# DiT block on one core: the MLP gate taken off TensorE and summed on VectorE and GpSimd

## The chip, the cores and the metric

The kernel runs on one core of a Trainium2 chip. The metric is the device time of one execution in microseconds (us); lower is better. A core has five engines with instruction queues of their own: TensorE (PE in the profile; its weight loads are PEld), VectorE (DVE), ScalarE (ACT), GpSimd (POOL) and SyncE (SP), which here issues most of the transfers (DMAs). They meet through semaphores.

## The reference

One transformer block whose normalisations are shifted and scaled, and whose two branches are gated, by six vectors per batch computed from `c`. B = 2, N = 256, D = 1152, two heads of 576, and an MLP of width F = 4608; everything is bf16.

```python
mod = (silu(c) @ w_mod).reshape(B, 6, 1, D)
shift_a, scale_a, gate_a, shift_m, scale_m, gate_m = [mod[:, i] for i in range(6)]
h = layernorm(x) * (1 + scale_a) + shift_a
q, k, v = split(h @ wqkv)
attn = softmax(einsum('bqhd,bkhd->bhqk', q, k) * Dh ** -0.5)
a = einsum('bhqk,bkhd->bqhd', attn, v).reshape(B, N, D) @ wo
x = x + gate_a * a
h2 = layernorm(x) * (1 + scale_m) + shift_m
m = gelu(h2 @ w_fc1) @ w_fc2
return x + gate_m * m
```

## The kernel before, in words

**The planner.** The kernel first collects its work as units, each with an engine, an estimated cost in ns and the memory that it reads and writes. `Sched._track` (L229) derives the dependences from that: in SBUF by overlapping bytes, in PSUM by whole banks (a VectorE read of a bank waits for the last TensorE unit that wrote to it). TensorE and SyncE keep the order in which the code lists their units. VectorE, ScalarE and GpSimd are ordered by a list scheduler (`schedule`, L281) with the given costs, save for a hand-written start on VectorE and ScalarE (`S.first`, L907). On the chip each engine then works through its list in order; the costs only decided that order.

**The memory.** One SBUF tensor, `arena`, is cut by hand into regions that are used several times (L572 to L649). `O_X` holds the input X, later T1 and OST, the work tiles of fc2's output (L618, L619). `O_A` holds the scale weights WSC, then WQ, then two of the four fc1 weight buffers and one MLP gate; `O_C` holds the shift weights WSH, then WV, then the other two fc1 buffers and the other gate. `O_R`, four pieces of W1 = 20,736 bytes per partition, holds WMODR, the weights of the four last modulation vectors (L599), and later WFC2, the weights of fc2 (L600); each quarter of WFC2 is nine k tiles. PSUM is eight banks of 512 f32 columns.

**The order of the work on TensorE.**
1. Head. Sixteen dummy matmuls of 512 columns (`warm`, L764), the transposes of normalised x for batch 0 (`xn_T(1)`, `xn_T(0)`), and between them the matmuls of the scale vector's first part (`mod_kt`, L769, L816 to L822), three k tiles for each of three weight loads. VectorE adds 1 (`sc1a`, L775) and makes the K operand (`hk`, L780) with ScalarE. Then K is projected, kt by kt, with the transposes of batch 1 in between (L828 to L836).
2. The rest of the scale vector ("scb"), the rest of K, the shift vector ("sh"), Q, the scores and softmax, and V (L837 to L1098).
3. `rows()` (L965), between V tiles: the four vectors gate_a, shift_m, scale_m and gate_m as rows. `quad_mm` (L878) runs four matmuls on four column quarters of the array; their stationary operand is the two silu columns ST and their moving operand the weights. 32-column groups of a vector go to the quarters in turn, so a vector is 288 columns wide in PSUM, at partitions 32q + b. shift_m and scale_m are transposed on VectorE into MT; the two gates go through ScalarE to ROWS, by Pool's DMA queue to a DRAM scratch, and back as a broadcast to all partitions (`gate_load`, L984).
4. Probabilities times V (`pv`, L991), the output projection (`wo_tile`, L1019) with the attention gate (L1031), the residual on GpSimd (L1032) and the second normalisation; `xn2_T` (L1039) transposes it and applies shift and scale (L1050 on VectorE, L1053 on ScalarE).
5. fc1 (`fc1_tile`, L1056): 36 tiles of 128 outputs, each evacuated by a GELU on ScalarE (L1063). VectorE has no work here.
6. fc2 (L1128 to L1144): four token tiles by three or, in the last, five pieces of columns, 36 matmuls each. VectorE multiplies by the gate into T1 (L1142) and adds x into OST (L1143); SyncE stores. fc1, fc2 and the output projection use six PSUM banks in rotation (`acc`, L1011).

**The loads** are listed for SyncE in the order of use; a load waits in the queue until the bytes that it overwrites were read for the last time, and everything behind it waits too. Fc1's weights come in nine loads of 512 columns through four buffers, so that the fifth and later ones wait for fc1 tiles (L1125).

Of the kernel before, what the change touches and what calls it, by code (L numbers as in the profile page):

```python
# [3 lines left out]

# [2 lines left out]


# [492 lines left out]
P = 128  # L501
# [15 lines left out]
def c_mm(n):  # L517
    return max(n / 2.4 + 2.5, 27.0)
# [26 lines left out]
def build_kernel(nc, x, c, wqkv, wo, w_mod, w_fc1, w_fc2, out):  # L545
# [5 lines left out]
    with (  # L551
# [4 lines left out]
        def sb(off, nbytes, dt=BF16):  # L556
            assert off % 4 == 0 and off + nbytes <= ARENA_BYTES, (off, nbytes)
            v = arena[:, off // 2:(off + nbytes) // 2]
            if dt == F32:
                v = v.bitcast(F32)  # L560
            return v

        def ps32(bank, c0=0, n=512):
            return psum[:, bank * 512 + c0: bank * 512 + c0 + n]
# [19 lines left out]
        def misc(nbytes):  # L584
            o = mo[0]
            mo[0] += (nbytes + 3) // 4 * 4
            assert mo[0] <= ARENA_BYTES
            return o

        def wmat(o, f):  # L590
            return sb(o, KT * f * 2).rearrange("p (k f) -> p k f", k=KT)
# [4 lines left out]
        WO = wmat(O_B, D)  # L596
        WSH = wmat(O_C, D)
        WV = wmat(O_C, D)
        WMODR = wmat(O_R, 4 * D)  # L599
        WFC2 = sb(O_R, 4 * W1).rearrange("p (k f) -> p k f", k=JT)  # L600
        WFC1 = [wmat(o, 512) for o in (O_A, O_A + 9216, O_C, O_C + 9216)]
        X = sb(O_X, 9216).rearrange("p (t d) -> p t d", t=4)
# [11 lines left out]
        GA = [sb(O_GA + b * 2304, 2304) for b in range(2)]  # L614
        GM = [sb(o + 18432, 2304) for o in (O_A, O_C)]
        XN2 = [sb(O_R + 4 * W1 - (i + 1) * 2304, 2304) for i in range(4)]
        ROWS = sb(O_R + 4 * W1 - 5 * 2304, 2304)[:, 0:576].rearrange("p (g n) -> p g n", g=2)
        T1 = [sb(O_X + i * 1536, 1536, F32) for i in range(3)]  # L618
        OST = [sb(O_X + 4608 + i * 768, 768) for i in range(3)]  # L619
        gt_offs = ([O_P + i * 1024 for i in range(8)] + [O_B + i * 1024 for i in range(20)]  # L620
# [8 lines left out]
        HC = sb(misc(72), 72, F32)  # L629
        ST = sb(misc(36), 36)  # L630
        SHA = sb(misc(1152), 1152, F32)
        SC1A = sb(misc(72), 72, F32)
        MT = sb(misc(2304), 2304, F32)
        SHM = MT[:, 0:288]
# [25 lines left out]
        def dma(dst, src, nbytes, name, is_out=False, eng="sp", run=4096):  # L660
            eff = 1.0 if run >= 4096 else (1.08 if run >= 2304 else (1.15 if run >= 1536 else (1.3 if run >= 1024 else 1.42)))
            return S.op(eng, 500.0 if eng == "sp" else 150.0, lambda e: e.dma_start(dst, src), reads=[src], writes=[dst],  # L662
                        name=name, dma_bytes=nbytes * eff, is_out=is_out)

        def dve(cost, fn, reads, writes, name):
            return S.op("dve", cost, fn, reads=reads, writes=writes, name=name)
# [50 lines left out]
        act(200, lambda e: e.activation(out=TH, in_=CT_PS, func=ACTF.Tanh, scale=0.5), [CT_PS], [TH], "c_tanh")  # L717
        dve(170, lambda e: e.tensor_scalar(out=HC, in0=CT_PS, scalar1=0.5, scalar2=None, op0=ALU.mult), [CT_PS], [HC], "c_half")
        dve(170, lambda e: e.scalar_tensor_tensor(out=ST, in0=TH, scalar=1.0, in1=HC, op0=ALU.add, op1=ALU.mult), [TH, HC], [ST], "c_silu")


        def ln_stats_dve(src, chunks, bn_t, mv_t, rstd_t, tag):
# [31 lines left out]
        def xn_T(t):  # L754
            b = t // 2
            S.unit("pe", KT * c_mm(128), "xnT_%d" % t)
            for kt in range(KT):
                tr(ps16(XB[b][kt // 4], (kt % 4) * 256 + (t % 2) * 128, 128), XN[:, t, kt * 128:(kt + 1) * 128], IDENT)
# [5 lines left out]
        def warm(n, tag):  # L764
            for i in range(n):
                S.unit("pe", 215.0, "warm_%s_%d" % (tag, i))
                mm(ps32(2), IDENT, Q4B, True, True)

        def mod_kt(W, kt, col0, name, fs=(0, 9)):  # L769
            S.unit("pe", (fs[1] - fs[0]) * 27.0, name)  # L770
            for f in range(*fs):
                mm(ps32(7, col0 + f * 2, 2), W[:, kt, f * 128:(f + 1) * 128], ST[:, kt:18:9], kt == 0 and f == fs[0], kt == KT - 1,
                   skip_group_check=True)

        def sc1a(ka, kb):  # L775
            m, o = ps32(7, 2 * ka, 2 * (kb - ka)), SC1A[:, 2 * ka:2 * kb]
            dve(170, lambda e: e.tensor_scalar(out=o, in0=m, scalar1=1.0, scalar2=None, op0=ALU.add), [m], [o], "sc1a_%d" % ka)  # L777
# [33 lines left out]
                copy_on(eng, QK[:, 9 + 2 * i:11 + 2 * i, b * 256:(b + 1) * 256], ps32(bank).rearrange("p (j t) -> p j t", j=2), 512, False,  # L811
                        "k_ev%d_%d" % (b, i))

        warm(14, "b")
        xn_T(1)
        for kt in range(0, 3):  # L816
            mod_kt(WSC, kt, 0, "sca_%d" % kt, (0, KC))
        xn_T(0)
        for kt in range(3, 6):
            mod_kt(WSC, kt, 0, "sca_%d" % kt, (0, KC))  # L820
        for kt in range(6, 9):
            mod_kt(WSC, kt, 0, "sca_%d" % kt, (0, KC))  # L822
        sc1a(0, KC)
        for kt in range(KC):
            hk(kt, 0, "act" if kt in (2, 4) else "dve")
# [52 lines left out]
        def quad_mm(bank, w, g0, g1, kt):  # L878
            n = 32 * (g1 - g0)
            for q in range(4):  # L880
                o = psum[32 * q:32 * q + 2, bank * 512:bank * 512 + n].rearrange("p (g c) -> p g c", c=32)
                mm(o, ST[:, kt:18:9], quads(w, g0, g1, q), kt == 0, kt == KT - 1, tile_position=(0, 32 * q))
# [4 lines left out]
            quad_mm(0, WSH[:, kt, :], 0, 9, kt)  # L887
        dma(WV, wqkv_v[:, :, 2 * D:3 * D], D * D * 2, "ld_wv", run=2304)
        for k0 in range(0, KT, 3):
            dma(WMODR[:, k0:k0 + 3, :], wmod_v[:, k0:k0 + 3, 2 * D:6 * D], 3 * P * 4 * D * 2, "ld_modr%d" % k0)  # L890
        MT1 = ps32(0, 0, 288)
        dve(c_dve_psum32(288), lambda e: e.transpose(SHA, MT1), [MT1], [SHA], "sha")  # L892
        for kt in range(KT):
# [66 lines left out]
            copy_on("act" if v_rr[0] % 2 else "dve", V[:, t, ci * CH:(ci + 1) * CH], o, CH, False, "v_ev%d_%d" % (t, ci))  # L960


        row_banks = (3, 4, 5)

        def rows():  # L965
            S.unit("pe", KT * 3 * c_mm(CH) + 200.0, "rows")
            for kt in range(KT):
                for r in range(3):
                    quad_mm(row_banks[r], WMODR[:, kt, :], 12 * r, 12 * r + 12, kt)
            copy_on("act", ROWS[:, 0, :], ps32(3, 0, 288), 288, False, "rows_ev0")  # L970
            for i, (bank, c0, n, d0) in enumerate(((3, 288, 96, 0), (4, 0, 384, 96), (5, 0, 96, 480))):
                src, dst = ps32(bank, c0, n), MT[:, d0:d0 + n]
                dve(c_dve_psum32(n), lambda e, src=src, dst=dst: e.transpose(dst, src), [src], [dst], "mt_%d" % i)
            sc, so = MT[:, 288:576].rearrange("p (k r) -> p k r", r=32)[:, :, 0:2], SC1M.rearrange("p (k b) -> p k b", b=2)
            dve(170, lambda e: e.tensor_scalar(out=so, in0=sc, scalar1=1.0, scalar2=None, op0=ALU.add), [sc], [so], "sc1m")
            copy_on("act", ROWS[:, 1, :], ps32(5, 96, 288), 288, False, "rows_ev1")
            for gi in range(2):
                for b in range(2):
                    dma(scratch[gi, b].rearrange("(k q c) -> q k c", q=4, c=32), ROWS[b:128:32, gi, :].rearrange("p (k c) -> p k c", c=32),
                        2304, "st_g%d%d" % (gi, b), eng="pool")  # L980
                if gi == 0:
                    gate_load(0, GA)

        def gate_load(gi, G):  # L984
            for b in range(2):
                dma(G[b], scratch[gi, b].partition_broadcast(P), P * D * 2, "ld_g%d%d" % (gi, b), eng="pool")


        PVB = [(0, 1, 2, 6, 7), (3, 4, 5, 0, 1)]
# [29 lines left out]
        def wo_tile(t, before={}):  # L1019
# [16 lines left out]
            dve(170, lambda e: e.scalar_tensor_tensor(out=nm, in0=m, scalar=-1.0, in1=rs, op0=ALU.mult, op1=ALU.mult), [m, rs], [nm], "nmr2_%d" % t)  # L1036
            act(1344, lambda e: e.activation(out=xn2, in_=x1, func=ACTF.Identity, scale=rs, bias=nm), [x1, rs, nm], [xn2], "xn2_%d" % t)  # L1037

        def xn2_T(t):  # L1039
            b = t // 2  # L1040
            xn2 = XN2[t]
            S.unit("pe", KT * c_mm(128), "xn2T_%d" % t)
            slot = [ps16(7, kt * 128, 128) if kt < 4 else ps16(6, (kt - 4) * 128, 128) for kt in range(KT)]
            for kt in range(KT):
                tr(slot[kt], xn2[:, kt * 128:(kt + 1) * 128], IDENT)
            for kt in range(KT):
                o, dst = slot[kt], H2T[:, kt, t * 128:(t + 1) * 128]
                s1, s2 = SC1M[:, kt * 2 + b:kt * 2 + b + 1], SHM[:, kt * 32 + b:kt * 32 + b + 1]
                if kt < (4 if t < 2 else 6):
                    dve(335, lambda e, o=o, dst=dst, s1=s1, s2=s2: e.tensor_scalar(out=dst, in0=o, scalar1=s1, scalar2=s2, op0=ALU.mult, op1=ALU.add),  # L1050
                        [o, s1, s2], [dst], "h2T_%d_%d" % (t, kt))
                else:
                    act(440, lambda e, o=o, dst=dst, s1=s1, s2=s2: e.activation(out=dst, in_=o, func=ACTF.Identity, scale=s1, bias=s2),  # L1053
                        [o, s1, s2], [dst], "h2T_%d_%d" % (t, kt))
# [41 lines left out]
        v_proj(3, 0)  # L1096
        v_proj(3, 1)
        v_proj(3, 2)  # L1098
        gate_load(1, GM)
        wfc1_load(2)  # L1100
        wfc1_load(3)
        for q4 in range(3):
            dma(WFC2[:, 9 * q4:9 * q4 + 9, :], wfc2_v[:, 9 * q4:9 * q4 + 9, :], 9 * P * D * 2, "ld_wfc2_%d" % q4, run=2304)
        for b in range(2):
            for h in range(2):
# [12 lines left out]
        for f in range(F0 - 2, F0):  # L1118
            fc1_tile(f, 0, 256)
        dma(WFC2[:, 27:36, :], wfc2_v[:, 27:36, :], 9 * P * D * 2, "ld_wfc2_3", run=2304)  # L1120
        for f in range(F0):
            fc1_tile(f, 256, 256)
        for f in range(F0, JT):
            if f % 4 == 0 and f // 4 >= 4:
                wfc1_load(f // 4)  # L1125
            fc1_tile(f, 0, 512)

        oi = 0  # L1128
        for t in range(4):
# [70 lines left out]
```

## Time and profile before

Three runs took 249.8, 249.31 and 249.6 us; the median is 249.6 us.

| | |
|---|---|
| profiled execution, device time | 249.6 us |
| its span, first to last instruction | 247.6 us |
| mean granted TensorE clock | 0.993 of full speed |
| chain: TensorE lines L681 and L684 | 93% of the span |
| chain: weights of the scale vector in the head | 3.4% of the span (8.32 us from 2.69) |
| from HBM | 50.14 MB |
| rows, on TensorE | 68.2 to 72.7 us |
| fc1, end of last GELU tile's matmuls | about 174 us |
| first fc2 output on VectorE | 180.48 us |

In the page's 40 slices each character is 6.19 us; a digit is the busy share, or the clock, in tenths. In a group line the columns are: line, engine, operation, output <- input, shapes, count, then busy us, mean ns of one (a matmul's includes its pipeline), then idle time of the engine before it and what ended that. L681 is the helper of all matmuls, L684 that of the transposes, L662 that of the DMAs, L676 and L678 those of PSUM evacuations. A timeline line has start, length, engine, line, operation, count, and in brackets the idle time before it with its releaser.

### The profile page before, as it was taken

To read this page: it belongs to the slowest core of one execution; us is meant where nothing else is said; L and a number is where in the kernel's file an instruction comes from. 1 tells how busy PE (TensorE), PEld (TensorE's weight loads), DVE (VectorE), ACT (ScalarE), POOL (GpSimd) and SP (SyncE) were. 2 spreads that over 40 slices of the span, in tenths; PEclk is the share of its full clock that TensorE was granted. 3 is DMA by queue.
4 is the path that set the end of the run, shared out by engine and by line. 5 is a ranking of instruction groups with operands and counts; after the bars stand their busy time and mean duration, and the time that the engine had idled before them with its cause. 6 is when DMAs were issued, how large, how long until landed. Compare 5 with 4: busy or idle time off the path is not lost.

```text
span 247.6 us, 4007 instructions
## 1 busy us (share of the span) xinstructions
PE 240.6 (97%) x1751; PEld 148.3 (60%) x1760; DVE 69.9 (28%) x179; ACT 64.1 (26%) x130; POOL 21.1 (9%) x35
## 2 busy tenths in 40 slices
PE   7699999999999999999999999999999999999995
PEld 2488854557656766798644444444566666666675
DVE  3634350356412678950000000000011122211112
ACT  5612340334311403985223322233000000000000
POOL 1300000000014268500000000000000000000000
PEclk9979999999999999999999999999999999999999
DMA  6999989999999999999945650000000000000000
GB/s 234 361 376 392 391 265 412 418 426 421 412 389 341 331 366 390 392 391 355 363 143 175 193 190 0 0 3 0 0 16 19 16 16 19 16 16 16 22 28 20
DMA packets 27708, 51.59 MB, mean 208 GB/s; under 512 B 1563, under 2 KB 15659, under 8 KB 26539
## 3 DMA queue, kind: packets, MB, share of 16 engines
q1 hardware_dynamic: 27216, 50.14, 56.1%
q0 software_dynamic: 448, 1.19, 1.5%
q8 instruction: 14, 0.23, 0.4%
q14 instruction: 3, 0.02, 0.0%
q10 hardware_dynamic: 27, 0.00, 0.0%
HBM read 50.14 MB, written 1.19 MB: 207 GB/s over the span
## 4 chain that ended last, share of the span: by engine, by line
PE 93%; DMA 3%; ACT 1%; SPq 1%; issue 0%; DVE 0%
PE psum L681 91%; DMA arena<-in_w_mod_dram 3%; PE psum L684 2%; ACT arena L1053 1%; SPq L662 1%; ACT arena L1037 1%; DVE arena L786 0%; DVE arena L1142 0%; DVE arena L1143 0%; DVE arena L777 0%
## 5 line engine op out<-in xcount | busy, mean ns | idle before, releaser
L681 PE MATMUL psum<-arena 128*128 128x384 bf16 (+8 forms) x1662 | 236.8, 312 | 3.7 <-POOL arena L704 1.4
L681 PEld LDWEIGHTS psum<-arena 128*128 128x128 bf16 (+1 forms) x1671 | 142.8, 97 | 93.3 <-issue 3.2
L1142 DVE TENSOR_TENSOR arena<-psum,arena 128x384 f32<-128x384 f32 (+3 forms) x14 | 7.0, 501 | 119.2 <-PE psum L681 119.2
L1063 ACT ACTIVATE arena<-psum 128x512 bf16<-128x512 f32 (+1 forms) x44 | 22.5, 522 | 42.6 <-PE psum L681 42.6
L676 ACT ACTIVATE arena<-psum 128x512 bf16<-128x512 f32 (+7 forms) x30 | 15.7, 546 | 35.6 <-PE psum L681 32.9
L678 DVE CAST arena<-psum 128x512 bf16<-128x512 f32 (+3 forms) x21 | 13.0, 627 | 26.4 <-PE psum L681 26.3
L1032 POOL TENSOR_TENSOR arena<-arena 128x384 f32<-128x384 f32 x12 | 10.9, 911 | 10.5 <-DVE arena L1031 9.3
L725 DVE BATCH_NORM_STATS2 arena<-arena 128x6 f32<-128x384 f32 (+1 forms) x18 | 9.5, 549 | 1.0 <-DMA arena<-in_x_dram 0.9
L684 PE MATMUL psum<-arena 128*128 128x128 bf16 (+1 forms) x89 | 7.5, 222 | 0.7 <-DVE arena L747 0.6
L684 PEld LDWEIGHTS psum<-arena 128*128 128x128 bf16 (+1 forms) x89 | 6.1, 100 | 3.2 <-DVE arena L747 1.1
L662 POOL DMA_DIRECT2D dit_scratch<-arena x4 | 2.7, 669 | 62.3 <-ACT arena L676 62.3
L1037 ACT ACTIVATE arena<-arena 128x1152 bf16<-128x1152 f32 x4 | 5.4, 1352 | 9.5 <-DVE arena L1036 9.5
L1031 DVE TENSOR_TENSOR arena<-psum,arena 128x384 f32<-128x384 f32 x12 | 6.6, 548 | 3.2 <-PE psum L681 2.4
L1143 DVE TENSOR_TENSOR arena<-arena 128x384 bf16<-128x384 f32 (+3 forms) x14 | 7.0, 500 | 0.5
L1053 ACT ACTIVATE arena<-psum,arena 128x128 bf16<-128x128 bf16 x16 | 6.1, 460 | 3.2 <-PE psum L684 2.5
L1050 DVE TENSOR_SCALAR arena<-psum,arena 128x128 bf16<-128x128 bf16 x20 | 5.5, 336 | 2.0 <-PE psum L684 1.8
L935 ACT ACTIVATE arena<-psum,arena 128x256 bf16<-128x256 f32 x8 | 3.7, 471 | 6.9 <-PE psum L681 5.4
L729 POOL TENSOR_TENSOR arena<-arena 128x1 f32<-128x1 f32 x6 | 3.3, 551 | 8.2 <-DVE arena L728 8.2
L898 ACT ACTIVATE arena<-arena 128x256 bf16<-128x256 bf16 x6 | 2.5, 496 | 3.3 <-DVE arena L892 3.3
L931 DVE TENSOR_REDUCE arena<-psum 128x2 f32<-128x512 f32 x4 | 2.8, 688 | 1.5 <-PE psum L681 1.5
L784 ACT ACTIVATE arena<-psum,arena 128x256 bf16<-128x256 bf16 x3 | 1.3, 472 | 7.0 <-PE psum L681 4.6
L786 DVE TENSOR_SCALAR arena<-psum,arena 128x256 bf16<-128x256 bf16 x7 | 2.4, 348 | 2.7 <-PE psum L684 1.4
(37 smaller groups left out, 33.4 us busy)
## 6 DMA issues: line engine op xcount, KB each, us to landing
arena<-in_w_mod_dram SPq DMA_DIRECT2D x3, 3456.0 KB, 26.0
arena<-in_w_fc_dram SPq DMA_DIRECT2D x9, 1152.0 KB, 8.7
arena<-in_w_fc_dram SPq DMA_DIRECT2D x4, 2592.0 KB, 20.5
arena<-in_wqkv_dram SPq DMA_DIRECT2D x18, 288.0 KB, 9.2
arena<-in_w_mod_dram SPq DMA_DIRECT2D x3, 864.0 KB, 12.8
arena<-in_wqkv_dram SPq DMA_DIRECT2D x1, 2592.0 KB, 10.0
arena<-in_wo_dram SPq DMA_DIRECT2D x1, 2592.0 KB, 40.3
arena<-in_w_mod_dram SPq DMA_DIRECT2D x3, 480.0 KB, 7.6
```

Source lines behind the costliest of these rows:

```text
L676: act(c_act(n), lambda e: e.activation(out=dst, in_=src, func=ACTF.Copy), [src], [dst], name)
L678: dve(c_dve_psum16(n) if psum16 else c_dve_psum32(n), lambda e: e.tensor_copy(dst, src), [src], [dst], name)
L681: S.instr(lambda e: e.matmul(o, lhsT=l, rhs=r, start=st, stop=sp, **kw), reads=[l, r], writes=[o])
L684: S.instr(lambda e: e.transpose(o, i_, idn), reads=[i_, idn], writes=[o])
L725: dve(550, lambda e, s=s, o=o: e.bn_stats(out=o, in_=s), [s], [o], "bn_%s_%d" % (tag, ci))
L1031: dve(550, lambda e, o=o, ga=ga, x1c=x1c: e.tensor_tensor(out=x1c, in0=o, in1=ga, op=ALU.mult), [o, ga], [x1c], "wo_t1_%d_%d" % (t, ci))
L1032: S.op("pool", 930, lambda e, xs=xs, x1c=x1c: e.tensor_tensor(out=x1c, in0=x1c, in1=xs, op=ALU.add), reads=[x1c, xs], writes=[x1c], name=" ...
L1037: act(1344, lambda e: e.activation(out=xn2, in_=x1, func=ACTF.Identity, scale=rs, bias=nm), [x1, rs, nm], [xn2], "xn2_%d" % t)
L1053: act(440, lambda e, o=o, dst=dst, s1=s1, s2=s2: e.activation(out=dst, in_=o, func=ACTF.Identity, scale=s1, bias=s2), [o, s1, s2], [dst], ...
L1063: act(c_act(ntok), lambda e: e.activation(out=dst, in_=o, func=ACTF.Gelu_apprx_tanh), [o], [dst], "gelu_%d_%d" % (f, tok0))
L1142: dve(c_dve_psum32(w), lambda e, o=o, gm=gm, t1=t1: e.tensor_tensor(out=t1, in0=o, in1=gm, op=ALU.mult), [o, gm], [t1], "fc2_t1_%d_%d" % ( ...
L1143: dve(c_dve_32(w), lambda e, t1=t1, x1c=x1c, ost=ost: e.tensor_tensor(out=ost, in0=t1, in1=x1c, op=ALU.add), [t1, x1c], [ost], "fc2_out_%d ...
```

## The change

- The MLP gate leaves `rows()`. WMODR has three vectors (gate_a, shift_m, scale_m) and starts at the second piece of `O_R`. A k tile is now 27 groups of 32 columns in two banks (14 and 13 groups: 448 and 416 columns) instead of 36 groups in three banks of 384. One gate goes through ROWS, the scratch and Pool's queue, not two.
- The gate's weights WGM are loaded to the first piece of `O_R`, where the first quarter of WFC2 will lie. That quarter's load moves from ahead of the attention's end to after the last fc1 load.
- `mlp_gate` (called before the second half of fc1 tiles): ACC is f32, 2 x 1152 per partition, over the whole of `O_X`, so over T1 and OST too. For each batch VectorE accumulates WGM times the silu value of each partition (ST32, a f32 copy of ST made on GpSimd) over nine k tiles; all 18 instructions stand behind the last VectorE instruction of the last `xn2_T`. Then GpSimd sums ACC over the 128 partitions and writes the sum to all of them, as GM.
- Seven more dummies: 15 instead of 14 ahead of `xn_T(1)`, one ahead of `xn_T(0)`, two ahead of the third and three behind the third group of scale matmuls.

```diff
-        WMODR = wmat(O_R, 4 * D)
+        WMODR = wmat(O_R + W1, 3 * D)
+        WGM = wmat(O_R, D)
+        ACC = sb(O_X, 9216, F32).rearrange("p (b d) -> p b d", b=2)
...
-        ROWS = sb(O_R + 4 * W1 - 5 * 2304, 2304)[:, 0:576].rearrange("p (g n) -> p g n", g=2)
+        ROWS = sb(O_R + 4 * W1 - 5 * 2304, 2304)[:, 0:288]
...
+        pool(200, lambda e: e.tensor_copy(ST32, ST), [ST], [ST32], "c_silu32")
...
-        warm(14, "b")
+        warm(15, "b")
         xn_T(1)
         for kt in range(0, 3):
             mod_kt(WSC, kt, 0, "sca_%d" % kt, (0, KC))
+        warm(1, "c")
         xn_T(0)
         for kt in range(3, 6):
             mod_kt(WSC, kt, 0, "sca_%d" % kt, (0, KC))
+        warm(2, "d")
         for kt in range(6, 9):
             mod_kt(WSC, kt, 0, "sca_%d" % kt, (0, KC))
+        warm(3, "e")
         sc1a(0, KC)
...
-            dma(WMODR[:, k0:k0 + 3, :], wmod_v[:, k0:k0 + 3, 2 * D:6 * D], 3 * P * 4 * D * 2, "ld_modr%d" % k0)
+            dma(WMODR[:, k0:k0 + 3, :], wmod_v[:, k0:k0 + 3, 2 * D:5 * D], 3 * P * 3 * D * 2, "ld_modr%d" % k0)
...
-        row_banks = (3, 4, 5)
+        row_parts = ((3, 0, 14), (4, 14, 27))
...
-                for r in range(3):
-                    quad_mm(row_banks[r], WMODR[:, kt, :], 12 * r, 12 * r + 12, kt)
-            copy_on("act", ROWS[:, 0, :], ps32(3, 0, 288), 288, False, "rows_ev0")
-            for i, (bank, c0, n, d0) in enumerate(((3, 288, 96, 0), (4, 0, 384, 96), (5, 0, 96, 480))):
+                for bank, g0, g1 in row_parts:
+                    quad_mm(bank, WMODR[:, kt, :], g0, g1, kt)
+            copy_on("act", ROWS, ps32(3, 0, 288), 288, False, "rows_ev")
+            for i, (bank, c0, n, d0) in enumerate(((3, 288, 160, 0), (4, 0, 416, 160))):
...
-            copy_on("act", ROWS[:, 1, :], ps32(5, 96, 288), 288, False, "rows_ev1")
-            for gi in range(2):
-                for b in range(2):
-                    dma(scratch[gi, b]..., ROWS[b:128:32, gi, :]..., 2304, "st_g%d%d" % (gi, b), eng="pool")
-                if gi == 0:
-                    gate_load(0, GA)
+            for b in range(2):
+                dma(scratch[0, b]..., ROWS[b:128:32, :]..., 2304, "st_g%d" % b, eng="pool")
+            for b in range(2):
+                dma(GA[b], scratch[0, b].partition_broadcast(P), P * D * 2, "ld_g%d" % b, eng="pool")
+
+        def mlp_gate(prev):
+            for b in range(2):
+                for kt in range(KT):
+                    o, w, s1 = ACC[:, b, :], WGM[:, kt, :], ST32[:, b * 9 + kt:b * 9 + kt + 1]
+                    if kt == 0:
+                        u = dve(1300, lambda e, o=o, w=w, s1=s1: e.tensor_scalar(out=o, in0=w, scalar1=s1, scalar2=None, op0=ALU.mult),
+                                [w, s1], [o], "gm_%d_%d" % (b, kt))
+                    else:
+                        u = dve(1300, lambda e, o=o, w=w, s1=s1: e.scalar_tensor_tensor(out=o, in0=w, scalar=s1, in1=o, op0=ALU.mult, op1=ALU.add),
+                                [w, s1, o], [o], "gm_%d_%d" % (b, kt))
+                    S.order_after(u, prev)
+                o, g = ACC[:, b, :], GM[b]
+                pool(12000, lambda e, o=o, g=g: e.partition_all_reduce(g, o, P, bass_isa.ReduceOp.add), [o], [g], "gm_sum%d" % b)
...
-        gate_load(1, GM)
         wfc1_load(2)
         wfc1_load(3)
-        for q4 in range(3):
+        dma(WGM, wmod_v[:, :, 5 * D:6 * D], D * D * 2, "ld_gm", run=2304)
+        for q4 in range(1, 3):
             dma(WFC2[:, 9 * q4:9 * q4 + 9, :], wfc2_v[:, 9 * q4:9 * q4 + 9, :], 9 * P * D * 2, "ld_wfc2_%d" % q4, run=2304)
...
         dma(WFC2[:, 27:36, :], wfc2_v[:, 27:36, :], 9 * P * D * 2, "ld_wfc2_3", run=2304)
+        mlp_gate(last_h2T[0])
         for f in range(F0):
             fc1_tile(f, 256, 256)
         for f in range(F0, JT):
             if f % 4 == 0 and f // 4 >= 4:
                 wfc1_load(f // 4)
             fc1_tile(f, 0, 512)
+
+        dma(WFC2[:, 0:9, :], wfc2_v[:, 0:9, :], 9 * P * D * 2, "ld_wfc2_0", run=2304)
```

More of the change, by code (lines that the diff above doesn't have):

```diff
@@ L5 @@
 import concourse.bass as bass
+from concourse import bass_isa
 from concourse import mybir
@@ L631, in build_kernel @@
         SHA = sb(misc(1152), 1152, F32)
+        ST32 = sb(misc(72), 72, F32)
         SC1A = sb(misc(72), 72, F32)
@@ L960, in v_proj @@
             copy_on("act" if v_rr[0] % 2 else "dve", V[:, t, ci * CH:(ci + 1) * CH], o, CH, False, "v_ev%d_%d" % (t, ci))
-        row_banks = (3, 4, 5)
+        row_parts = ((3, 0, 14), (4, 14, 27))
         def rows():
-            S.unit("pe", KT * 3 * c_mm(CH) + 200.0, "rows")
+            S.unit("pe", KT * 864 / 2.4 + 500.0, "rows")
             for kt in range(KT):
-                for r in range(3):
-                    quad_mm(row_banks[r], WMODR[:, kt, :], 12 * r, 12 * r + 12, kt)
-            copy_on("act", ROWS[:, 0, :], ps32(3, 0, 288), 288, False, "rows_ev0")
-            for i, (bank, c0, n, d0) in enumerate(((3, 288, 96, 0), (4, 0, 384, 96), (5, 0, 96, 480))):
+                for bank, g0, g1 in row_parts:
+                    quad_mm(bank, WMODR[:, kt, :], g0, g1, kt)
+            copy_on("act", ROWS, ps32(3, 0, 288), 288, False, "rows_ev")
+            for i, (bank, c0, n, d0) in enumerate(((3, 288, 160, 0), (4, 0, 416, 160))):
                 src, dst = ps32(bank, c0, n), MT[:, d0:d0 + n]
@@ L975, in rows @@
             dve(170, lambda e: e.tensor_scalar(out=so, in0=sc, scalar1=1.0, scalar2=None, op0=ALU.add), [sc], [so], "sc1m")
-            copy_on("act", ROWS[:, 1, :], ps32(5, 96, 288), 288, False, "rows_ev1")
-            for gi in range(2):
-                for b in range(2):
-                    dma(scratch[gi, b].rearrange("(k q c) -> q k c", q=4, c=32), ROWS[b:128:32, gi, :].rearrange("p (k c) -> p k c", c=32),
-                        2304, "st_g%d%d" % (gi, b), eng="pool")
-                if gi == 0:
-                    gate_load(0, GA)
-        def gate_load(gi, G):
-            for b in range(2):
-                dma(G[b], scratch[gi, b].partition_broadcast(P), P * D * 2, "ld_g%d%d" % (gi, b), eng="pool")
+            for b in range(2):
+                dma(scratch[0, b].rearrange("(k q c) -> q k c", q=4, c=32), ROWS[b:128:32, :].rearrange("p (k c) -> p k c", c=32),
+                    2304, "st_g%d" % b, eng="pool")
+            for b in range(2):
[13 more added lines that the diff above has]
+                pool(12000, lambda e, o=o, g=g: e.partition_all_reduce(g, o, P, bass_isa.ReduceOp.add), [o], [g], "gm_sum%d" % b)
         PVB = [(0, 1, 2, 6, 7), (3, 4, 5, 0, 1)]
@@ L1037, in wo_tile @@
             act(1344, lambda e: e.activation(out=xn2, in_=x1, func=ACTF.Identity, scale=rs, bias=nm), [x1, rs, nm], [xn2], "xn2_%d" % t)
+        last_h2T = [None]
         def xn2_T(t):
@@ L1049, in xn2_T @@
                 if kt < (4 if t < 2 else 6):
-                    dve(335, lambda e, o=o, dst=dst, s1=s1, s2=s2: e.tensor_scalar(out=dst, in0=o, scalar1=s1, scalar2=s2, op0=ALU.mult, op1=ALU.add),
+                    last_h2T[0] = dve(335, lambda e, o=o, dst=dst, s1=s1, s2=s2: e.tensor_scalar(out=dst, in0=o, scalar1=s1, scalar2=s2, op0=ALU.mult, op1=ALU.add),
                         [o, s1, s2], [dst], "h2T_%d_%d" % (t, kt))
```

## The prediction

> **What bounds the kernel now.** I read the page from the top: TensorE is busy for 97% of the span, the chain of work that ended last is 93% TensorE, and no other engine is over 28%. A change can shorten the kernel only by taking TensorE work away, by closing a TensorE gap, or by making TensorE run faster; the slices show where its clock was low.
>
> ```profile
> span 247.6 us, 4007 instructions
> PE 240.6 (97%) x1751; PEld 148.3 (60%) x1760; DVE 69.9 (28%) x179; ACT 64.1 (26%) x130; POOL 21.1 (9%) x35
> ...
> PE   7699999999999999999999999999999999999995
> ...
> PEclk9979999999999999999999999999999999999999
> ...
> PE 93%; DMA 3%; ACT 1%; SPq 1%; issue 0%; DVE 0%
> ```
>
> The third slice (12.4 to 18.6 us) is the only one with a low clock. The timeline of TensorE shows the four gaps ahead of the K projection (the first 128x256 row), in brackets:
>
> ```profile
> 2.51 4.75 PE L681 MATMUL psum<-arena 128*128 128x512 bf16 x14
> 7.88 0.68 PE L684 MATMUL psum<-arena 128*128 128x128 bf16 x9 [0.61 <-DVE arena L747]
> 8.51 0.55 PE L681 MATMUL psum<-arena 128*128 128x2 bf16 x15
> 8.92 0.66 PE L684 MATMUL psum<-arena 128*128 128x128 bf16 x9
> 9.79 0.55 PE L681 MATMUL psum<-arena 128*128 128x2 bf16 x15 [0.21 <-DMA arena<-in_w_mod_dram]
> 11.06 0.55 PE L681 MATMUL psum<-arena 128*128 128x2 bf16 x15 [0.72 <-DMA arena<-in_w_mod_dram]
> 12.37 3.48 PE L681 MATMUL psum<-arena 128*128 128x256 bf16 x16 [0.76 <-DVE arena L786]
> ```
>
> Windows of 0.2 us (window, TensorE busy, clock, DMA share, GB/s) place the drop: 0.81 in the first of these rows makes it 12.52 us, 0.66 in the last makes the return 15.93 us. That is 3.41 us at half clock.
>
> ```profile
> 12.40:12.60 0.20, 0.20 (x2) 0.81 1.03 403
> ...
> 15.60:15.80 0.20, 0.20 (x4) 0.50 1.12 353
> 15.80:16.00 0.20, 0.20 (x5) 0.66 1.08 343
> ```
>
> The groups by shape give the rows, the Pool price and the long idle stretch of VectorE:
>
> ```profile
> L681 PE MATMUL psum<-arena 128*2 128x384 bf16 x108 | 4.6, 326 | 0.0
> ...
> L1142 DVE TENSOR_TENSOR arena<-psum,arena 128x384 f32<-128x384 f32 x11 | 6.1, 558 | 115.5 <-PE psum L681 115.5
> L1143 DVE TENSOR_TENSOR arena<-arena 128x384 bf16<-128x384 f32 x11 | 6.1, 557 | 0.4
> ```
>
> **Rows, 4 vectors to 3.** The 108 matmuls are 9 k tiles by 3 banks by 4 column quarters, and the four quarters run side by side: 27 groups in 4.6 us. A full 384-column matmul of the V projection takes 1.46 us / 9 = 0.163 us, so a group costs what one does, 0.423 ns a column. After, a k tile streams 448 + 416 = 864 columns instead of 1152: 9 x 288 x 0.423 ns = **1.10 us** less. Bounds: by instruction count, 36 of 108 at 4.6/108 us is 1.5 us; 1.1 is the lower end and I take it, because columns fit both rows. It is on the path: TensorE goes straight on to V. Beside it go one evacuation on ScalarE, some 100 ns of VectorE transposes, and two stores and two loads of Pool's queue. The attention gate arrives sooner; its first user waited 0.6 us for it at 86.4, but TensorE did not wait for that user, so this is worth 0.
>
> **Seven more dummies.** One costs 0.21 us at full clock (the last five of the 14 took about 1.0). They go into the four gaps: 0.21 into 0.61; 0.21 ahead of the second transposes (which then end some 0.16 us before the 9.79 load); 0.43 into 0.72; 0.65 into 0.76, while VectorE makes the first K operand, which waits for the last scale matmul and not for the dummies. So by themselves they cost **0**. Without that cover, seven cost 1.5 us at full clock and 3.0 at half.
>
> What they may change is the clock. Going back from the drop in steps of 3.41 us, the stretch 9.11 to 12.52 has TensorE busy for 1.73 us (51%) and is followed by half clock; 5.70 to 9.11 has 2.79 us (82%) and is not. After, the first of these gains the last two sets (1.08 us) and the transposes pushed into it, and reaches 2.8 to 3.0 us: as much as the stretch that held. Counted by columns streamed alone (0.21 per dummy, 0.056 per transpose), the one that held had about 2.0, the one that lost 0.5, the new one 1.7; nearer the one that held. I take it that the clock holds. Then 12.37 to 17.66, 24 K matmuls and 18 transposes in 5.29 us, would take 24 x 0.109 + 18 x 0.056 = 3.62: **1.67 us** less. Bounds: 0 and 1.7.
>
> [...]
>
> What is late next? The operands of the K matmuls end on VectorE and ScalarE at 13.05, 13.56 and 13.95, and at full clock they are needed at 13.24, 14.6 and 14.3. By issue and time to landing, the second part of the scale weights lands at about 19.1 (needed at 19.4 after the shift), the shift weights at 29.1 (needed at 31), the last modulation weights at 69.2, now a quarter smaller. The gain should survive, with the scale weights as the tightest.
>
> **The gate on VectorE and Pool.** The f32 two-input rows of L1143 (225 ns for 64 columns, 557 for 384) extend to 1.35 us for 1152, so 18 instructions are 24.4 us (the first of each nine may be cheaper). They start behind the last modulated transpose, at 112.0, and end at 124.2 and 136.4 in before's time. VectorE's next work is at 180.5: hidden.
>
> Pool's sum over partitions is in no trace. From below: one pass over 1152 columns by the L1032 row (0.911 us for 384) is 2.7 us. From above: seven halving passes are 19 us, 127 passes in sequence 347 us. The planner's 12.0 in the diff lies by the seven passes (its 930 ns for L1032 stands against a measured 911), and I take 12. The sums then end at 136 and 148.
>
> When does it hurt? T1 and OST lie in ACC, so the first output addition of fc2 also waits for the *second* sum, with VectorE's queue behind it. Tile 0 and its bank are free by then; TensorE has six banks, and stalls only when its eighth fc2 tile needs the bank of the second: 174.2 + 7 x 5.85 = 215.2. The second sum must end by 214: 124.2 + 2S < 214, S < 45 us. At 12 the price is **0**.
>
> [...]
>
> **Loads.** The SP queue issues the gate weights where the first quarter of fc2's weights stood, with the same bytes, and they are due at about 102, ahead of 112. That quarter goes behind the last fc1 load, which is issued at 143.5, and behind the gate's last read (136.4). With 20.5 us, the median of such loads in the busy stretch, it lands at 164.4; fc2 starts at 174.2. The output stores behind it in SP's queue begin at 181.7. Price 0, with 9.8 us to spare. The ST32 copy is on Pool while it idles, 1.4 to 6.4 us: 0.
>
> **Sum.** 249.6 - 1.10 - 1.67 = **246.8 us**. The profiled execution took 249.6 (span 247.6 and 2.0 around it), which is also the median of the runs. About 0.2% (0.5 us) can be told from no change.
>
> **Rivals.**
> 1. *The clock drops all the same*, because 1.7 us of streaming is too little or the edges fall elsewhere. The dummies stay in the gaps, rows alone count: 248.5.
> 2. *The dummies run at half clock* (an edge before them). The two take 0.85 in a gap of 0.72 and the three 1.28 in 0.76, so K starts about 0.65 late: 249.6 - 1.1 + 0.65 = 249.1, within 0.2%. The full clock in all gaps now speaks against it.
> 3. *Pool's sum becomes the end.* Beyond S = 45 us each us costs two; in before's time the second sum ends at 124.2 + 2S, and 33.4 us of fc2 follow (247.6 - 215.2, and 1 for VectorE). At 347 us this gives 852 + 2 us; at 60 us 279.6. Against it: seven passes or the planner's figure are less than half of the limit.
> 4. *A load is late*: the fc2 quarter over 30 us, as one load of the modulation weights behind a full queue was (34). It would end at 177.9, 3.7 us late: 250.5. Against it: the DMA share is 0.23 and lower from 140 us on.
>
> **Chances.** Forecast 0.62; rival 1 0.22; rival 2 0.05; rival 3 0.08; rival 4 0.03. So faster 0.84, same 0.05, slower 0.11. The forecast alone spans 246.3 to 247.3 (1.5 us for rows; 0.5 lost again at the scale weights); with rival 1 it holds 0.84, to 248.7. That is the range.
>
> **What would show it.** Clock: no slice under 9 at 12 to 18 us, and the K matmuls at 109 ns. Rows: 72 matmuls in about 3.4 us. Gate: VectorE busy 24 us from about 109, two Pool rows ending before 150, no wait of fc2 other than for TensorE. The prediction is wrong if the clock falls again, if the saved time returns as a TensorE wait on a weight load before 35 us, or if a Pool sum takes over 45 us.

## The result and the profile after

The changed kernel takes 257.13 us (median of 4 runs, 256.33 to 258.27) against 249.45 us before: 1.034 times as long, with a 95% interval of 1.030 to 1.038. The forecast was 246.8. The profiled execution of the changed kernel took 256.33 us, with a span of 254.2.

The page after, its span, its busy times, the slices of TensorE, GpSimd and the clock, and the chain by engine:

```profile
span 254.2 us, 3965 instructions
PE 238.4 (94%) x1721; PEld 147.1 (58%) x1731; DVE 92.4 (36%) x196; ACT 63.6 (25%) x129; POOL 33.9 (13%) x34
...
PE   0099999999999999999999999999999999999995
...
POOL 0021000000002127550000993000000000000000
PEclk9999999999999999999999999999999999999999
...
PE 92%; issue 5%; ACT 1%; DVE 0%; POOL 0%; POOLq 0%
```

TensorE is busy for 2.2 us less, and the slice with the low clock is gone, as forecast. (For the first dummies the clock column is no guide: in both kernels they start 0.43 us apart and the later ones 0.216, and it reads 1.00 for all of them.) But the first two slices are empty: 12.2 us in which TensorE does nothing. The chain has 5% of "issue", which was 0%; that is time in which an engine waited for nothing that the profile shows. The timeline of GpSimd says where, in one line of before and two of after:

```profile
1.06 0.29 POOL L704 TENSOR_SCALAR_AFFINE_SELECT arena<-arena 128x128 bf16<-128x128 bf16 x1
```

```profile
0.93 0.10 POOL L712 MEMSET arena<- 128x1 f32 x1
11.85 0.28 POOL L708 TENSOR_SCALAR_AFFINE_SELECT arena<-arena 128x128 bf16<-128x128 bf16 x1 [10.82 <-issue]
```

L708 (L704 before) makes the identity matrix, which every dummy and every transpose on TensorE uses. Before, it ran at 1.06 us; now GpSimd stands still for 10.82 us ahead of it, behind nothing but a memset. The end of GpSimd's list, in the same view, shows the new sums:

```profile
112.76 0.55 POOL L734 TENSOR_TENSOR arena<-arena 128x1 f32<-128x1 f32 x1 [1.13 <-DVE arena L733]
140.08 14.74 POOL L1002 PARTITION_ALL_REDUCE arena<-arena  x2 [26.77 <-DVE arena L998]
```

And TensorE's timeline, to be read beside the seven rows that the prediction shows:

```profile
12.19 1.03 PE L685 MATMUL psum<-arena 128*128 128x512 bf16 x2 [12.19 <-POOL arena L708]
13.16 0.19 PE L688 MATMUL psum<-arena 18*128 18x18 bf16 x1
13.28 4.78 PE L685 MATMUL psum<-arena 128*128 128x512 bf16 x15
17.89 0.67 PE L688 MATMUL psum<-arena 128*128 128x128 bf16 x9
18.40 0.78 PE L685 MATMUL psum<-arena 128*128 128x2 bf16 x16
```

The weight loads of `rows()`, before and after:

```profile
68.24 4.16 PEld L681 LDWEIGHTS psum<-arena 128*2 128x2 bf16 x108 [0.32 <-issue]
75.87 3.02 PEld L685 LDWEIGHTS psum<-arena 128*2 128x2 bf16 x72 [0.32 <-issue]
```

The two profiled executions, stage by stage (times from the TensorE and weight-load timelines and the chains):

| Stage | before | after | difference |
|---|---|---|---|
| start to first matmul | 1.41 | 12.19 | +10.78 |
| to the first K matmul (12.37; 21.66) | 10.96 | 9.47 | -1.49 |
| to the end of the last transposes between the K matmuls (17.83; 25.46) | 5.46 | 3.80 | -1.66 |
| rows, first weight load to that of the next V tile (68.24 to 72.73; 75.87 to 79.26) | 4.49 | 3.39 | -1.10 |
| sum | | | +6.53 |
| span | 247.6 | 254.2 | +6.6 |

So both forecast gains are there, 1.66 for the clock and 1.10 for the rows. The late start costs 10.8, of which 1.5 come back: by then both the weights (waits of 0.21 and 0.72 us before) and the normalised x (0.61) are there. The stages by themselves don't show that the dummies held the clock, since the late start closes most gaps too; a pair of runs below does.

### The profile page after: what moved, and what is told of

It is laid out like the page before. It is cut to its first block, busy times and chain, and to the rows that moved or that the text cites. A ratio compares the mean times of both kernels' runs of the same rounds, so it can differ in the third digit from the quotient of the medians.

```text
span 254.2 us, 3965 instructions
## 1 busy us (share of the span) xinstructions
PE 238.4 (94%) x1721; PEld 147.1 (58%) x1731; DVE 92.4 (36%) x196; ACT 63.6 (25%) x129; POOL 33.9 (13%) x34
## 4 chain that ended last, share of the span: by engine, by line
PE 92%; issue 5%; ACT 1%; DVE 0%; POOL 0%; POOLq 0%
PE psum L685 90%; PE psum L688 2%; ACT arena L1071 1%; ACT arena L1053 1%; DVE arena L791 0%; POOL arena L708 0%; DVE arena L1163 0%; DVE arena L1164 0%; POOL arena L707 0%; DVE arena L782 0%; POOL arena L712 0%; POOLq L708 0%; POOLq L1206 0%
## 5 line engine op out<-in xcount | busy, mean ns | idle before, releaser
L685 PE MATMUL psum<-arena 128*128 128x384 bf16 (+8 forms) x1632 | 235.2, 312 | 13.0 <-POOL arena L708 12.2
L685 PEld LDWEIGHTS psum<-arena 128*128 128x128 bf16 (+1 forms) x1642 | 141.6, 97 | 101.9 <-POOL arena L708 12.2
L998 DVE SCALAR_TENSOR_TENSOR arena<-arena 128x1152 f32<-128x1152 bf16 x16 | 21.4, 1414 | 0.0
L1002 POOL PARTITION_ALL_REDUCE arena<-arena x2 | 14.7, 7412 | 26.8 <-DVE arena L998 26.8
L1048 POOL TENSOR_TENSOR arena<-arena 128x384 f32<-128x384 f32 x12 | 10.9, 911 | 13.4 <-DVE arena L1047 12.2
L666 POOL DMA_DIRECT2D dit_scratch<-arena x2 | 1.6, 786 | 59.4 <-ACT arena L680 59.4
```

Of the source, the lines that this page charges most:

```text
L685: S.instr(lambda e: e.matmul(o, lhsT=l, rhs=r, start=st, stop=sp, **kw), reads=[l, r], writes=[o])
L998: u = dve(1300, lambda e, o=o, w=w, s1=s1: e.scalar_tensor_tensor(out=o, in0=w, scalar=s1, in1=o, op0=ALU.mult, op1=ALU.add), [w, s1, o], ...
L1002: pool(12000, lambda e, o=o, g=g: e.partition_all_reduce(g, o, P, bass_isa.ReduceOp.add), [o], [g], "gm_sum%d" % b)
L1048: S.op("pool", 930, lambda e, xs=xs, x1c=x1c: e.tensor_tensor(out=x1c, in0=x1c, in1=xs, op=ALU.add), reads=[x1c, xs], writes=[x1c], name=" ...
```

## The experiments

Three theories were set against each other. **R, residency:** GpSimd's sum needs other code than its ordinary operations; the execution ends with the sum's code in place, and the next one fetches the ordinary code ahead of its first ordinary operation, the identity. **L:** any program with two sets of code loads at the start. **D:** the dummies or the silu copy hold the start. R is suggested by a pair of GpSimd instructions named MODIFY_POOL_CONFIG, which the views above don't print but the stored traces hold: both kernels have one pair ahead of the identity, and the changed kernel has a second at 113.51 us, ahead of the sums (140.08). Before, the identity starts 0.10 us behind its pair (0.97 us); in the changed kernel 10.81 us behind it (1.045 us). That what is fetched is code is the author's inference from this name and from the runs below; no view shows it.

### The change with one ordinary operation at the end

```diff
-                pool(12000, lambda ...: e.partition_all_reduce(g, o, P, bass_isa.ReduceOp.add), [o], [g], "gm_sum%d" % b)
+                u = pool(12000, lambda ...: e.partition_all_reduce(g, o, P, bass_isa.ReduceOp.add), [o], [g], "gm_sum%d" % b)
+            t = pool(300, lambda e: e.tensor_tensor(out=SUMS[:, 0:1], in0=NHALF, in1=NHALF, op=ALU.add), [NHALF], [SUMS[:, 0:1]], "tail")
+            S.order_after(t, u)
```

> The changed kernel with one more GpSimd instruction of a single column (an addition, as the block's own GpSimd additions are) behind the second sum. Theory R (residency): the 10.8 us ahead of the identity at the start are GpSimd fetching the code for its ordinary operations, because the previous execution ended with the code of the sum in place. The added addition brings the ordinary code back while fc2 runs, so the next start finds it: the first TensorE instruction at about 1.4 us, 249.5 - 1.1 (rows) - 1.7 (clock) = 246.7 us, 246.2 to 247.5. Rival L (a load at the start, whatever was in place): any program with two sets of GpSimd code loads at the start; then 257 us, as the change. Rival D (the dummies or the silu copy on GpSimd hold the start): 257 us too.

Measured: 246.48 us (246.38 to 246.82); ratio to before 0.989, interval 0.987 to 0.992. GpSimd's timeline:

```profile
1.32 0.29 POOL L708 TENSOR_SCALAR_AFFINE_SELECT arena<-arena 128x128 bf16<-128x128 bf16 x1 [0.29 <-POOL arena L712]
...
130.27 14.74 POOL L1002 PARTITION_ALL_REDUCE arena<-arena  x2 [26.76 <-DVE arena L998]
154.47 0.18 POOL L1003 TENSOR_TENSOR arena<-arena 128x1 f32<-128x1 f32 x1 [9.46 <-issue]
```

The wait has moved. The 10.82 us ahead of the identity are gone, and 9.46 us of the same unexplained kind stand ahead of the added operation, in the middle of fc1, where nobody waits for GpSimd. Both sums are as before. One instruction of 0.18 us that computes nothing of use takes off 10 us. R holds in where it puts the wait; L and D fall.

### The change without the sum

```diff
-                pool(12000, lambda ...: e.partition_all_reduce(g, o, P, bass_isa.ReduceOp.add), [o], [g], "gm_sum%d" % b)
+                pool(3000, lambda e, o=o, g=g: e.tensor_copy(g, o), [o], [g], "gm_sum%d" % b)
```

> The changed kernel with GpSimd's sum over partitions left out: the gate is only copied from the accumulator to its bf16 place, so the MLP gate is not summed over partitions. All else stays. Theory R and rival L: without the sum there is one set of GpSimd code and no wait at the start: 246.7 us, 246.2 to 247.5, the 10.8 us gone. Rival D: the dummies and the silu copy are still there, so 257 us.

Measured: 246.68 us (246.46 to 246.85), with the identity at 1.05 us:

```profile
1.05 0.29 POOL L708 TENSOR_SCALAR_AFFINE_SELECT arena<-arena 128x128 bf16<-128x128 bf16 x1
```

The dummies and the silu copy are innocent, and it is the sum that brings the wait. With the sum and the closing operation the kernel is as fast as without the sum: its 14.7 us are hidden.

### The kernel before with one small sum

```diff
+        last = [u for u in S.units if u.name == "rstd_ln2_3"][0]
+        u = pool(12000, lambda e: e.partition_all_reduce(SHA[:, 0:32], SHA[:, 32:64], P, bass_isa.ReduceOp.add), [SHA[:, 32:64]], [SHA[:, 0:32]], "lone_sum")
+        S.order_after(u, last)
```

> The kernel before with one sum over partitions of 32 columns on dead scratch, as the last GpSimd instruction, whose result nobody reads. Theory R and rival L: the start waits about 10.8 us ahead of the identity. Behind it the weight loads have landed, so that 0.9 us of waits for them vanish: 249.5 + 10.8 - 0.9 = 259.4 us with the clock drop of before, 257.7 without it. Rival D: 249.5 us, no wait at the start.

Measured: 257.74 us (256.34 to 258.52); ratio 1.034, interval 1.029 to 1.038. A sum of 0.55 us, 120 us into the kernel and read by nobody, costs 8 us:

```profile
11.93 0.28 POOL L705 TENSOR_SCALAR_AFFINE_SELECT arena<-arena 128x128 bf16<-128x128 bf16 x1 [10.90 <-issue]
...
112.97 0.55 POOL L730 TENSOR_TENSOR arena<-arena 128x1 f32<-128x1 f32 x1 [1.14 <-DVE arena L729]
120.33 0.55 POOL L1130 PARTITION_ALL_REDUCE arena<-arena  x1 [6.80 <-issue]
```

Here the sum's operands were there in time, so its own wait of 6.80 us is bare; in the change such a wait doesn't show beside the 26.77 us for VectorE. This kernel has none of the added dummies, and all four of its executions have a granted clock of 1.0, against 0.993 in the profiled execution of before: here the late start went with the full clock, without dummies.

### The same with the ordinary operation behind it

```diff
         S.order_after(u, last)
+        t = pool(300, lambda e: e.tensor_tensor(out=SUMS[:, 0:1], in0=NHALF, in1=NHALF, op=ALU.add), [NHALF], [SUMS[:, 0:1]], "tail")
+        S.order_after(t, u)
```

> The kernel before with the lone sum of 32 columns and the closing addition behind it. Theory R: the ordinary code is back before the execution ends, no wait at the start, 249.4 us, although the sum and both code loads are still in the program. Rival (a sum anywhere in the program makes the start load code): 257.7 us, as without the addition.

Measured: 248.49 us (247.15 to 250.05); ratio 1.001, interval 0.997 to 1.004. Half of its ten executions took 247.2 to 247.7 us, at a granted clock of 1.0, and half 249.2 to 250.1, at 0.993; the next section has the same two kinds. GpSimd's timeline:

```profile
1.32 0.29 POOL L705 TENSOR_SCALAR_AFFINE_SELECT arena<-arena 128x128 bf16<-128x128 bf16 x1 [0.29 <-POOL arena L709]
...
110.84 0.55 POOL L1130 PARTITION_ALL_REDUCE arena<-arena  x1 [6.28 <-issue]
121.36 0.18 POOL L1132 TENSOR_TENSOR arena<-arena 128x1 f32<-128x1 f32 x1 [9.96 <-issue]
```

The waits are 6.28 us ahead of the sum and 9.96 ahead of the addition, and no such wait is ahead of the identity (1.32 us). So it isn't that a sum stands in the program, but what stands last in it.

### The clock: the change with closing operation, without and with the dummies

```diff
-        warm(15, "b")
+        warm(14, "b")
...
-        warm(1, "c")
...
-        warm(2, "d")
...
-        warm(3, "e")
```

> The changed kernel with the closing addition on GpSimd, but with the head's dummies as before (14, and none in the three other places). Theory C (the prediction's clock step): without the dummies the stretch of 3.41 us ahead of the K projection falls short again and K starts at half clock: 249.4 - 1.1 = 248.3 us, with some 3.4 us of half clock in the trace from about 12 us. Rival (the clock does not hang on the dummies, it varies by itself): 246.5 us as with them, or times of both kinds.

> The changed kernel with the closing addition, once more, as the partner of the one without the dummies: 246.5 us, full clock from the first K matmul on.

Measured: without, 248.05 us (246.31 to 248.58; ratio to before 0.995, 0.992 to 0.999); with, 246.63 us (246.31 to 246.98; ratio 0.9915, 0.988 to 0.995). Single executions tell more than the medians. Without the dummies, 4 of 12 took 246.3 to 246.9 us (granted clock 1.0) and 8 took 247.9 to 248.6 (0.993); with them, all 9 took 246.3 to 247.0 (0.999 to 1.0). The profiled one without them, at 248.28, shows the drop, in windows of 0.5 us (TensorE busy, clock, DMA share, GB/s):

```profile
12.50:13.00 0.50, 0.50 (x6) 0.74 1.06 416
13.00:13.50 0.50, 0.50 (x4) 0.50 1.01 377
...
15.50:16.00 0.50, 0.50 (x6) 0.50 1.10 348
16.00:16.50 0.50, 0.50 (x6) 0.84 1.11 354
```

Half clock from about 12.74 to 16.16, 3.4 us again. Theory C and its rival both have a part: the clock varies by itself without the dummies, and with them it didn't in any of these nine executions. The medians of the pair differ by 1.4 us.

### The dummies alone, twice

```diff
-        warm(14, "b")
+        warm(15, "b")
...
+        warm(1, "c")
...
+        warm(2, "d")
...
+        warm(3, "e")
```

> The kernel before with the seven more dummies and nothing else. Theory R: no wait at the start; the clock holds through the K projection: 249.5 - 1.7 = 247.8 us, no half clock at 12 to 16 us. If the clock falls all the same: 249.5 us. Rival D: the start is held and the time is over 255 us.

> The kernel before with the seven dummies alone, once more, since its first median (248.63) was 1.1 us above what the clock should give. Theory C: its times are those of the faster group of the kernel before, 247.4 to 248.0, and the first runs were late at the last output stores by chance. Rival (without the smaller weights of the rows something else comes late by about 1 us): again 248.1 to 249.2, with full clock, and the lost time to be found in the trace.

Measured: 248.63 us (ratio 0.9975, 0.995 to 1.000), then 248.82 us (248.09 to 249.33; ratio 1.001, 0.998 to 1.004). The first has the K projection at full clock (8 matmuls in 1.04 us, granted clock 1.0), and its fc1 starts 2.03 us sooner than before (108.18 against 110.21). But its span is only 1.1 us shorter. The second keeps its clock too (1.0); its transposes had to wait 1.73 us for the normalised x, and its span is 0.5 us longer than that of the first. The end of both is late at one place: the output store of 56 KB (3.2 us in the first run, 1.7 before), by issue and time to landing of the last stores (of the second run, and then of the change with the closing operation):

```profile
out_dram<-arena SPq DMA_DIRECT2D x1, 56.0 KB, 3.4
out_dram<-arena SPq DMA_DIRECT2D x1, 24.0 KB, 2.3
```

```profile
out_dram<-arena SPq DMA_DIRECT2D x1, 56.0 KB, 1.5
out_dram<-arena SPq DMA_DIRECT2D x1, 24.0 KB, 1.5
```

From the end of the last matmul to the end of the span it is 3.5 us there (243.52 to 247.0) against 2.4 before (245.16 to 247.6). That is the 1 us. Why this program's store is slow isn't known: its stores are those of before. The rival holds, in that the loss is in the trace and isn't chance; its cause stays open.

### The sums made eight times as long

```diff
-                u = pool(12000, lambda ...
+                for _ in range(8):
+                    u = pool(12000, lambda ...
```

> The changed kernel with the closing addition, each sum done eight times over with the same result: S = 8 x 7.4 = 59 us, so that the last sum ends at about 130.3 + 118 = 248 us. Theory W (the prediction's limit: fc2's first addition into OST waits for the second sum, VectorE stands behind it, and TensorE stops ahead of its eighth fc2 tile at about 212 us): span 248 + 33.4 = 281.6, time 283.5 us. Rival (only the gate's own readers wait; the first batch goes on): TensorE runs on to its thirteenth tile and stops at 241 us at most, so the time ends at about 248 + 10 = 258 us. Second rival (a sum repeated is much cheaper than the first): 246.5 us.

Measured: 275.44 us, but not by the planned way: the planner, with sums of 96 us in its sight, put VectorE's multiply-adds in between the last shift-and-scale instructions, and TensorE stood still three times in fc1, 3.7 us in all. The forecast was 8 us too long all the same: a repeated sum takes 6.8 us (102.24 for 15), so that the last ended at 239.1 and not at 248. So it was done again, with the cost 1500 in place of 12000.

> As the eightfold sums before, with a smaller cost given to the planner, so that VectorE's order is that of the changed kernel and fc1 is not held (there, the multiply-adds had moved in between the last shift-and-scale instructions and cost TensorE 3.7 us). Sixteen sums of 6.9 us from 130.3: the last ends at about 240.5. Theory W (the first addition into OST waits for the last sum, VectorE stands behind it, and TensorE stops once six banks are full): TensorE stops between 206 and 212, its eighth fc2 tile starts at about 241, span 240.5 + 33.4 = 274, time 276 us. Rival (only the readers of each gate wait for it): 258 us at most. Second rival (VectorE and GpSimd hold up fc1 by their SBUF traffic): fc2 starts later than 171.5.

Measured: 276.24 us, span 274.1. VectorE's timeline:

```profile
233.59 0.56 DVE L1166 TENSOR_TENSOR arena<-psum,arena 128x384 f32<-128x384 f32 x1 [102.26 <-POOL arena L1003]
240.40 0.56 DVE L1167 TENSOR_TENSOR arena<-arena 128x384 bf16<-128x384 f32 x1 [6.26 <-POOL arena L1003]
```

TensorE's timeline:

```profile
106.79 99.48 PE L685 MATMUL psum<-arena 128*128 128x256 bf16 x558
234.20 37.29 PE L685 MATMUL psum<-arena 128*128 128x384 bf16 x288 [27.93 <-DVE arena L1166]
```

The first multiplication by the gate waits for the first batch's last sum, and the first addition into OST waits for the second batch's, as theory W has it; TensorE stops at 206.3 for 27.93 us, once six banks are full. The sums of the two batches alternate here: the multiplication goes on at 233.59, when the fifteenth of the sixteen ends, where eight sums of the first batch in a row would have ended at about 185. So the first batch's gate is late too, and TensorE stops ahead of its seventh fc2 tile and not of its eighth. Behind the stop the seventh tile ended at about 241.9, two tiles of 5.85 us ahead of the ninth, which VectorE reads at 253.79; it took 7.7 us. Half clock in its first 3.7 us would give that, an estimate from these numbers; the mean granted clock of the execution is 0.95. By its end the next bank was free; there was no second stop. In 5.85 us the tile would have ended at about 240.1 (234.2 + 5.85), and TensorE would have waited until 241.4, the end of the second multiplication, as theory W has it. So the time agrees to 0.5 us, though by a somewhat other path.

Fc1 isn't held by the 110 us of GpSimd work beside it: fc2's first six tiles end at 206.3, as 171 + 6 x 5.85 gives. The second rival falls: in this run VectorE's and GpSimd's work beside fc1 costs TensorE nothing that shows.

## Why the prediction was wrong

- **Rows: right.** 1.10 us forecast, 1.10 measured, by columns and not by instructions.
- **Dummies and clock: right in what they do, and the size needs a word.** The stretch ahead of K held its clock in every profiled execution with the dummies (mean granted clock 0.999 to 1.0), the pair without and with them shows that they do it, and the K stage gained 1.66 us against the 1.67 forecast. But the profiled execution of before belonged to the slower of two kinds. In one job's runs of before, nine lie at 247.4 to 248.0 us (granted clock 1.0) and the others from 248.9 up (0.986 to 0.993): some executions keep the clock without help. So against the median the dummies are worth less than 1.7 us. The two groups lie 1.5 us apart. The three times of before that stood with the prediction, 249.31 to 249.8, are all of the slower kind; the fourth, 247.69, came with the result. How much work a stretch needs to hold the clock, and whether the clock goes by steps of 3.41 us with edges, as the prediction's stretches and first two rivals take it, no run shows. Measured are the drops: 12.52 to 15.93 us before, about 12.74 to 16.16 in the profiled execution without the dummies, and none in those with them.
- **Gate, multiply-adds: right in price.** 1.33 us each in sequence (21.35 / 16) against 1.35. Their order was another: the two batches alternate, so that the first sum starts at 140.08 us, some 9 us later than the forecast 124.2 moved by the 6.5 us that this part is late. **Sums: right that they are hidden; the 12 us was too long**: 7.4 each (14.74 / 2). **The limit: right that fc2's first addition waits for the last sum**; with eightfold sums 276 us were forecast and 276.24 measured, by a somewhat other path, as said.
- **Loads: right.** (The prediction's landing at 164.4 is a slip: 143.5 + 20.5 is 164.0.) No wait of TensorE on a load behind the head. The moved quarter of fc2's weights was issued at 151.6 and landed 12.4 us later, at 164.0; fc2 started at 180.7.
- **The step that failed: "At 12 the price is 0."** I priced the sum by its duration, between two points where nobody waits for GpSimd, and asked only when its end would be late. What else the new operation does to GpSimd was put at nothing, without a reason. What it costs stands at the other end of the kernel: 10.82 us ahead of the identity, by theory R for the code that the sum leaves behind, on the path because all of TensorE's head hangs on it. None of the four rivals had it; the one on the sum had the wrong place and the wrong mechanism. With that wait moved off the path by the closing operation, the time is 246.48 us, against the 246.8 of the prediction's sum.
- **What could have told.** Not the trace of before: it has no sum, and the identity starts 0.10 us behind its one MODIFY_POOL_CONFIG pair. The runs show a wait on both sides of a sum: bare, 6.80 and 6.28 us ahead of it, and ahead of the next ordinary operation 10.82 and 10.90 us at the start, 9.46, 9.96 and 10.77 behind the sums, 7.58 and 6.95 behind the long ones. And the question to ask was not when the new operation runs, but what runs next on that engine; next comes the following execution.

## What to carry to other kernels

GpSimd's sum over partitions, the one such operation tried here, has two prices, its own time (7.4 us for 1152 columns) and the waits on its engine on both sides of it: 6.28 and 6.80 us ahead of it where it stood bare, and 6.95 to 10.90 us ahead of the next ordinary operation, even across the end of the kernel. That these are a change of code is the inference above. Look for the same with other operations of this kind, and put an ordinary operation behind it where the engine is idle: here that turned 257.1 us into 246.5 us, faster than both kernels. The memsets at the start of the changed kernel ran ahead of the wait (the last at 0.93 us), so a memset may not do as closing operation; no run tried one. When timing a change of 1 us, look at single executions: two groups 1.5 us apart in the kernel before make any median of it a matter of luck.

## What the runs showed of the hardware

- GpSimd's sum over 128 partitions, f32 in, takes 0.55 us for 32 columns and 7.4 for 1152 (6.9 when it is repeated, 110.17 for 16): 5.7 to 6.1 ns a column from the two widths, well below the prediction's upper estimate of seven passes, 19 us.
- The wait ahead of the next ordinary operation is not a constant:

| where | wait, us |
|---|---|
| start of the changed kernel | 10.82 |
| start of the kernel with one small sum | 10.90 |
| behind the sums, beside fc1 (two runs) | 9.46, 10.77 |
| behind the one small sum | 9.96 |
| behind the long sums, beside fc2 (two runs) | 7.58, 6.95 |

The two shortest are the two beside fc2. What makes the difference no run shows.

- With the closing operation the identity still starts 0.26 us later than in the kernel before, which has no sum (1.32 against 1.06 us).
